# Decode block on one core: the first weight load as two half-partition loads on two queues

## The chip, the cores and the metric

The kernel runs on one core of a Trainium2 chip. The metric is device time in microseconds (us), the median of repeated runs; lower is better. The profile is of one execution.

## The reference

One decode step of a transformer block for 8 sequences, float32 throughout: a pre-norm grouped-query attention over the last 1,024 cached positions, then a pre-norm gated feed-forward part, both with residual additions.

```python
W = min(4096, max(256, Sk // 4))              # Sk = 4096, so W = 1024
q = (layernorm(x) @ wq)                       # x: 8 x 1024, wq: 1024 x 4096, 32 heads of 128
scores = q . k[last W] * Dh ** -0.5           # k, v: 8 x 4 x 4096 x 128, 8 query heads share a k head
o = softmax(scores) . v[last W]
h = x + o @ wo                                # wo: 4096 x 1024
g, u = layernorm(h) @ w_gate, layernorm(h) @ w_up     # 1024 x 3584 each
out = h + (gelu(g) * u) @ w_down              # 3584 x 1024
```

With 8 rows of activations, every weight and every cache line is read once and used for 8 rows: some 111 MB come in, and only 0.13 MB go out.

## The kernel before

The whole kernel is a stream of large loads from HBM into two equal buffers in SBUF, `w0` and `w1` (`wbuf`), each 128 partitions by 64 KB. Each load fills the buffers in turn: `wq` (two halves of the columns, `wq0` and `wq1`), `kt` (the transposed keys, two), `v` (two), `wo` (two), `gu` (gate and up weights, four), and `dn` with `ends` (the down weights, in pieces that get smaller towards the end). All loads are issued by SyncE (SP), in that order; the chip carries them out on 16 DMA engines. `load` gives a transfer a wait on the last matmul that reads the buffer (`free[i]`), so a load is issued as soon as the buffer's earlier content has been used, while the other buffer's load is still under way.

A load of 128 x 16384 floats is 8.39 MB; in the trace it is 128 packets of 64 KB, one for each partition, that is 8 for each of the 16 DMA engines.

There is no scheduler. `Flow.run` and `Flow.move` (line 87) issue instructions in the order in which the code is written, and put a semaphore wait ahead of an instruction where its engine has not yet seen the value that it needs. Each transfer has a semaphore of its own, which its landing raises by 16.

The start of the program, where the change lies, goes like this. SP issues `wq0` into `w0`, then `x` (8 partitions of 4 KB), then `wq1` into `w1`. VectorE (DVE) waits for `x`, takes its layer norm (lines 181 to 197, with one square root on ScalarE, ACT, line 188), TensorE (PE) transposes it (line 171), and DVE copies it out as `ln_t` (line 201). Then PE multiplies it by `wq0` into the PSUM bank `acc` (line 215, 32 matmuls, 64 in the trace's records), later by `wq1` into `tb`. The end of the first of these groups frees `w0`, and SP may issue `kt0`; the end of the second frees `w1` for `kt1`. From there on each stage has this form: a load lands, PE works through it, the buffer is free for the load after next.

Of the kernel before, what the change touches and what calls it, by code (L numbers as in the profile page):

```python
# [7 lines left out]
P = 128  # L8
# [6 lines left out]
NC = D // P  # L15
NQ = 4
# [17 lines left out]
class Flow:  # L34
# [42 lines left out]
    def run(self, engine, make, *waits, mark=True):  # L77
        ins = self.start(engine, make, waits)
        if not mark:
            return None  # L80
        self.done[engine] += 1
        ins.then_inc(self.own[engine], 1)
        return self.own[engine], self.done[engine]

    def move(self, name, out, src, *waits, engine="sync"):
        s = self.sem(name)
        self.start(engine, lambda e: e.dma_start(out, src), waits).then_inc(s, 16)  # L87
        return s, 16


def decode_block(nc, x, wq, kt, v, wo, gu, dn, ends, outs):
# [9 lines left out]
    run, move = fl.run, fl.move  # L101
# [4 lines left out]
    def sb(name, *shape):  # L106
        return nc.alloc_sbuf_tensor(name, list(shape), F32).ap()
# [9 lines left out]
    def buffer():  # L117
        i = turn[0] % 2
        turn[0] += 1
        return i, wbuf[i]  # L120

    def load(src, name, letters, **sizes):

        i, buf = buffer()
        n = 1
        for s in src.shape[1:]:
            n *= s
        t = buf[:, 0:n].rearrange(f"p ({letters}) -> p {letters}", **sizes)
        return t, move(name, t, src, free[i]), i
# [3 lines left out]
    acc = bank("acc", N)  # L133

    x_sb = sb("x_sb", B, D)
    wq_t = [load(wq[0], "wq0", "c n", c=NC)]
    x_in = move("x", x_sb, x)
    wq_t.append(load(wq[1], "wq1", "c n", c=NC))


    ident = sb("ident", P, P)
# [24 lines left out]
    def transposes(pt, src, n, ready, clear, rows=P):  # L166

        t = pt[:, 0:n * rows].rearrange("p (n r) -> p n r", n=n)
        tok = None
        for i in range(n):  # L170
            tok = run("tensor", lambda e, i=i: e.transpose(  # L171
                t[:, i, :], src[:, i * P:(i + 1) * P], ident[:rows, :rows]),
                id_ok, ready, clear, mark=(i == n - 1))
        return t, tok

    def layernorm_t(src, ready, name, clear):

        bn = sb(name + "_bn", B, D // N, 6)
        tok = None
        for i in range(D // N):  # L180
            tok = run("vector", lambda e, i=i: e.bn_stats(bn[:, i], src[:, i * N:(i + 1) * N]), ready)
        mv, ve, sd, r0, r1, r2, rs = (
            sb(f"{name}_{n}", B, k) for n, k in
            (("mv", 2), ("ve", 1), ("sd", 1), ("r0", 1), ("r1", 1), ("r2", 1), ("rs", 1))
        )
        tok = run("vector", lambda e: e.bn_aggr(mv, bn), tok)
        tok = run("vector", lambda e: e.tensor_scalar(ve, mv[:, 1:2], EPS, None, op0=ALU.add), tok)  # L187
        tok = run("scalar", lambda e: e.activation(sd, ve, AF.Sqrt), tok)  # L188
        tok = run("vector", lambda e: e.reciprocal(r0, sd), tok)

        tok = run("vector", lambda e: e.scalar_tensor_tensor(
            r1, r0, r0, ve, op0=ALU.mult, op1=ALU.mult), tok)
        tok = run("vector", lambda e: e.tensor_scalar(
            r2, r1, -0.5, 1.5, op0=ALU.mult, op1=ALU.add), tok)
        tok = run("vector", lambda e: e.tensor_mul(rs, r0, r2), tok)
        xn = sb(name + "_xn", B, D)
        tok = run("vector", lambda e: e.tensor_scalar(  # L197
            xn, src, mv[:, 0:1], rs, op0=ALU.subtract, op1=ALU.mult), tok)
        pt, tok = transposes(ta, xn, NC, tok, clear, B)
        xt = sb(name + "_t", P, NC, CP, B)  # L200
        tok = run("vector", lambda e: e.tensor_copy(  # L201
            xt, pt.unsqueeze(2).to_broadcast([P, NC, CP, B])), tok)
        return [xt[:, c].rearrange("p r b -> p (r b)") for c in range(NC)], tok

    xt, x_ok = layernorm_t(x_sb, x_in, "ln1", None)
# [4 lines left out]
    for hf in range(2):  # L210
        w, w_in, wb = wq_t[hf]
        q_ps = (acc, tb)[hf]
        for c in range(NC):
            for j in range(NQ):
                tok = run("tensor", lambda e, c=c, j=j: e.matmul(  # L215
                    q_ps[32 * j:32 * j + 32, :], xt[c], w[:, c, j * N:(j + 1) * N],
                    start=(c == 0), stop=(c == NC - 1)),
                    w_in, x_ok, mark=(c == NC - 1 and j == NQ - 1))
        free[wb] = tok
        q_sb = sb(f"q{hf}", P, N)  # L220
        tok = run("vector", lambda e: e.tensor_scalar(q_sb, q_ps, scale, None, op0=ALU.mult), tok)
        acc_free = tok
        qt, tok = transposes(ta, q_sb, N // P, tok, ta_free)

        for s in range(2):
            ta_free = run("vector", lambda e, s=s: e.tensor_copy(
                qz[hf][:, s].rearrange("p (b m) -> p b m", b=B)[:, :, 0:REP].rearrange(
                    "p b (k i) -> p b k i", k=2),
                qt.rearrange("p i (s k m) -> p s m k i", s=2, k=2)[:, s, 0:B]), tok, zero[hf])
        q_ok.append(ta_free)  # L230
# [3 lines left out]
    for hf in range(2):  # L234
        s_ps = big[hf]
        k_t, k_in, wb = load(kt[hf], f"kt{hf}", "s b k", s=2, b=B)
        for b in range(HB):
            for k0 in range(0, W, N):
                for r in range(NQ):
                    s, half = divmod(r, 2)  # L240
# [37 lines left out]
    for hf in range(2):  # L278
# [8 lines left out]
        for c in range(KC):  # L287
            for r in range(NQ):
                s, half = divmod(r, 2)
# [4 lines left out]
                    v_in, ta_free, ya_free, mark=(c == KC - 1 and r == NQ - 1))  # L294
# [15 lines left out]
    for hf in range(2):  # L310
# [3 lines left out]
        w, w_in, wb = load(wo[hf], f"wo{hf}", "h n", h=2 * REP)  # L314
# [26 lines left out]
    for k, nb in enumerate(SETS):  # L341
        pair = big[1 - k].rearrange("p (s n) -> p s n", s=2)
        clear = (ps[1][1], h_ok)[k]
        for s in range(2):
            w, w_in, wb = load(gu[k][s], f"gu{k}_{s}", "c n", c=NC)
            for c in range(NC):
                for j in range(nb):
# [3 lines left out]
                        w_in, ht_ok, clear, mark=(c == NC - 1 and j == nb - 1))  # L351
# [19 lines left out]
    for n in (HEAD, DF // P - HEAD):  # L371
        i, buf = buffer()
# [29 lines left out]
    for q in range(0, first, 2):  # L402
        for i in range(NQ):
# [7 lines left out]
                mark=(q == first - 2 and i == NQ - 1))  # L411
# [27 lines left out]
    mark = sb("mark", 1, 1)  # L439
# [82 lines left out]
```

## Time and profile before

| | us |
|---|---|
| median of 3 runs | 266.21 (266.11 to 266.24) |
| the profiled execution | 266.2 |
| its span, first to last instruction | 264.9 |
| busy PE / PE weight loads / DVE / ACT / GpSimd | 137.6 / 39.8 / 23.2 / 10.7 / 3.2 |
| first load issued, DVE begins on x | 0.74, 23.18 |
| wq1 landed, kt0 issued | 42.33, 37.90 |

The profile names DMA queues by numbers: q1 is the queue on which SP issues, q8 brings instructions in. "DMA share" in a row of a view by windows is the time of the packets that begin in the window, over 16 engines and the window's length; "GB/s" are the bytes of the same packets over the window's length. A packet is counted where it begins, so that a short window can show a share above 1, and share x length x 16 / number of packets is the mean time of one packet. `SPq` is SyncE's queue of transfers; a time "to landing" runs from issue to the semaphore of the transfer.

### The profile page before, as it was taken

To read this page: it belongs to the slowest core of one execution; us is meant where nothing else is said; L and a number is where in the kernel's file an instruction comes from. 1 tells how busy PE (TensorE), PEld (TensorE's weight loads), DVE (VectorE), ACT (ScalarE), POOL (GpSimd) and SP (SyncE) were. 2 spreads that over 40 slices of the span, in tenths; PEclk is the share of its full clock that TensorE was granted. 3 is DMA by queue.
4 is the path that set the end of the run, shared out by engine and by line. 5 is a ranking of instruction groups with operands and counts; after the bars stand their busy time and mean duration, and the time that the engine had idled before them with its cause. 6 is when DMAs were issued, how large, how long until landed. Compare 5 with 4: busy or idle time off the path is not lost.

```text
span 264.9 us, 2030 instructions
## 1 busy us (share of the span) xinstructions
PE 137.6 (52%) x946; PEld 39.8 (15%) x946; DVE 23.2 (9%) x55; ACT 10.7 (4%) x16; POOL 3.2 (1%) x11
## 2 busy tenths in 40 slices
PE   0000886804905906807707708719409585686696
PEld 0000321201201301302202202112102121121122
DVE  0004010100010020300200100260000200010001
ACT  1002000000010020110000000020000000000000
POOL 4000000000000000000000000000000000000000
PEclk9999997955965895965975956986966979599599
DMA  8998998999899989998999999999999998999994
GB/s 317 475 445 351 475 475 366 428 465 475 356 445 465 468 346 445 468 445 376 455 465 435 388 435 475 406 416 445 468 408 393 438 460 379 438 426 421 426 409 154
DMA packets 3192, 111.44 MB, mean 421 GB/s; under 512 B 360, under 2 KB 616, under 8 KB 1008
## 3 DMA queue, kind: packets, MB, share of 16 engines
q1 hardware_dynamic: 3184, 111.31, 97.9%
q8 instruction: 7, 0.11, 0.2%
q14 instruction: 1, 0.01, 0.0%
HBM read 111.18 MB, written 0.13 MB: 420 GB/s over the span
## 4 chain that ended last, share of the span: by engine, by line
DMA 75%; PE 22%; SPq 0%; issue 0%; DVE 0%; ACT 0%
DMA w<-gu 19%; DMA w<-wq 15%; DMA w<-kt 12%; DMA w<-wo 11%; DMA w<-v 11%; DMA w<-dn 8%; PE big L348 7%; PE big L243 4%; PE tb L290 3%; PE tb L215 3%; PE ya L318 3%; PE ya L406 1%; SPq L87 0%; DVE d L413 0%; ACT o_fin L437 0%
## 5 line engine op out<-in xcount | busy, mean ns | idle before, releaser
L348 PE MATMUL big<-w,ln_t 128*32 128x512 f32 x224 | 36.3, 734 | 21.6 <-DMA w<-gu 21.6
L243 PE MATMUL big<-w,qz 128*32 128x512 f32 x128 | 19.0, 762 | 20.5 <-DMA w<-kt 20.5
L318 PE MATMUL ya<-w,ot 128*32 128x512 f32 x128 | 18.2, 734 | 19.5 <-DMA w<-wo 19.5
L406 PE MATMUL ya<-w,at 128*32 128x512 f32 x104 | 17.4, 690 | 5.3 <-DMA w<-dn 5.3
L171 PE MATMUL ta<-ident,ln_xn 8*128 8x8 f32 x16 | 1.8, 236 | 31.7 <-DVE ln_xn L197 31.7
L348 PEld LDWEIGHTS big<-w,ln_t 128*32 128x32 f32 x224 | 9.1, 132 | 47.3 <-issue 26.0
L290 PE MATMUL tb<-w,pt 128*32 128x512 f32 x64 | 9.2, 741 | 9.7 <-DMA w<-v 9.7
L290 PE MATMUL acc<-w,pt 128*32 128x512 f32 x64 | 8.6, 700 | 8.5 <-DMA w<-v 8.5
L215 PE MATMUL tb<-w,ln_t 128*32 128x512 f32 x64 | 8.8, 711 | 3.1 <-DMA w<-wq 3.1
L243 PEld LDWEIGHTS big<-w,qz 128*32 128x32 f32 x128 | 4.9, 137 | 34.0 <-issue 23.4
L215 PE MATMUL acc<-w,ln_t 128*32 128x512 f32 x64 | 9.5, 761 | 0.5 <-DVE ln_t L201 0.5
L318 PEld LDWEIGHTS ya<-w,ot 128*32 128x32 f32 x128 | 5.0, 132 | 31.3 <-issue 31.3
L406 PEld LDWEIGHTS ya<-w,at 128*32 128x32 f32 x104 | 4.3, 124 | 17.5 <-issue 9.8
L171 PEld LDWEIGHTS ta<-ident,ln_xn 8*128 8x128 f32 x16 | 1.6, 188 | 32.6 <-DVE ln_xn L197 32.6
L359 DVE TENSOR_TENSOR hm<-ge,big 128x512 f32<-128x512 f32 (+1 forms) x2 | 1.4, 685 | 57.0 <-PE big L348 57.0
L252 DVE TENSOR_REDUCE nmax<-big 128x1 f32<-128x1024 f32 x2 | 2.4, 1224 | 36.3 <-PE big L243 36.3
L290 PEld LDWEIGHTS tb<-w,pt 128*32 128x32 f32 x64 | 2.6, 134 | 15.6 <-issue 15.6
L254 ACT ACTIVATE p<-big,nmax 128x1024 f32<-128x1024 f32 x2 | 2.2, 1114 | 65.9 <-DVE nmax L252 65.9
L290 PEld LDWEIGHTS acc<-w,pt 128*32 128x32 f32 x64 | 2.4, 126 | 14.1 <-issue 14.1
L188 ACT ACTIVATE ln_sd<-ln_ve 8x1 f32<-8x1 f32 x2 | 0.4, 203 | 84.0 <-DVE ln_ve L187 84.0
L215 PEld LDWEIGHTS tb<-w,ln_t 128*32 128x32 f32 x64 | 2.3, 127 | 8.8 <-issue 5.5
L215 PEld LDWEIGHTS acc<-w,ln_t 128*32 128x32 f32 x64 | 2.3, 135 | 7.0 <-issue 6.3
(72 smaller groups left out, 48.2 us busy)
## 6 DMA issues: line engine op xcount, KB each, us to landing
w<-gu SPq DMA_DIRECT2D x2, 6144.0 KB, 22.0
w<-dn SPq DMA_DIRECT2D x2, 4096.0 KB, 20.1
w<-dn SPq DMA_DIRECT2D x2, 2048.0 KB, 17.7
w<-dn SPq DMA_DIRECT2D x1, 1024.0 KB, 22.0
w<-dn SPq DMA_DIRECT2D x1, 512.0 KB, 22.8
w<-ends SPq DMA_DIRECT2D x2, 256.0 KB, 23.0
out<-o_fin SPq DMA_DIRECT2D x2, 64.0 KB, 1.6
w<-wq SPq DMA_DIRECT2D x2, 31.5
```

Of the source, the lines that this page charges most:

```text
L171: tok = run("tensor", lambda e, i=i: e.transpose(t[:, i, :], src[:, i * P:(i + 1) * P], ident[:rows, :rows]), id_ok, ready, clear, mark=(i ...
L188: tok = run("scalar", lambda e: e.activation(sd, ve, AF.Sqrt), tok)
L215: tok = run("tensor", lambda e, c=c, j=j: e.matmul(q_ps[32 * j:32 * j + 32, :], xt[c], w[:, c, j * N:(j + 1) * N], start=(c == 0), stop=(c ...
L243: tok = run("tensor", lambda e: e.matmul(s_ps[32 * r:32 * r + 32, k0:k0 + N], qz[hf][:, s, c0:c0 + 32], k_t[:, s, half * HB + b, k0:k0 + N ...
L252: tok = run("vector", lambda e: e.tensor_reduce(out=nmax, in_=s_ps, axis=AX.X, op=ALU.max, negate=True), tok)
L254: p_ok = run("scalar", lambda e: e.activation(p_sb, s_ps, AF.Exp, bias=nmax, accum_out=tot), tok)
L290: tok = run("tensor", lambda e: e.matmul(o3[32 * r:32 * r + 32], pt[:, c, 32 * r:32 * r + 32], v_t[:, s, c, half * HB:(half + 1) * HB, :], ...
L318: tok = run("tensor", lambda e: e.matmul(ya[32 * r:32 * r + 32, :], ot[:, 2 * hf * REP + h + e2].rearrange("p r b -> p (r b)"), w[:, h + e ...
L348: tok = run("tensor", lambda e: e.matmul(pair[32 * j:32 * j + 32, s, :], ht[c], w[:, c, j * N:(j + 1) * N], start=(c == 0), stop=(c == NC ...
L359: tok = run("vector", lambda e: e.tensor_mul(hm[:rows], ge[:rows], pair[:rows, 1, :]), tok, g_ok)
L406: tok = run("tensor", lambda e: e.matmul(ya[32 * r:32 * r + 32, :], at[:, q + e2, :], rows_of(q + e2)[:, ch * N:(ch + 1) * N], start=(q == ...
```

## The change

The first load, `wq0`, becomes two transfers: partitions 0 to 63 from SP's queue, partitions 64 to 127 from ACT's queue, both into the same buffer as before, each with a semaphore of its own. The first matmul on `wq0` waits for both. Nothing else is changed: `x` and `wq1` stay on SP, behind the first half now.

```diff
     x_sb = sb("x_sb", B, D)
-    wq_t = [load(wq[0], "wq0", "c n", c=NC)]
+
+    i, buf = buffer()
+    first_w = buf.rearrange("p (c n) -> p c n", c=NC)
+    half = P // 2
+    wq0_in = [move(f"wq0_{k}", first_w[k * half:(k + 1) * half], wq[0][k * half:(k + 1) * half],
+                   engine=("sync", "scalar")[k]) for k in range(2)]
+    wq_t = [(first_w, wq0_in, i)]
     x_in = move("x", x_sb, x)
-    wq_t.append(load(wq[1], "wq1", "c n", c=NC))
+    w1, w1_in, i = load(wq[1], "wq1", "c n", c=NC)
+    wq_t.append((w1, [w1_in], i))
...
                     q_ps[32 * j:32 * j + 32, :], xt[c], w[:, c, j * N:(j + 1) * N],
                     start=(c == 0), stop=(c == NC - 1)),
-                    w_in, x_ok, mark=(c == NC - 1 and j == NQ - 1))
+                    *w_in, x_ok, mark=(c == NC - 1 and j == NQ - 1))
```

ACT at the start of the program, before. A row is a line of the code, the operation, and what it writes from what; `ln_sd` is the square root in the layer norm, `p` the exponentials of the scores.

```order
L188 ACT_TABLE_LOAD
L188 ACTIVATE ln_sd<-ln_ve 8x1
L254 ACT_TABLE_LOAD
L254 ACTIVATE p,tot<-big,nmax 128x1024 x2
L284 COPY pt<-ya 128x512 x2
```

ACT at the same place with the change (the line numbers after the insertion are 7 higher):

```order
L87 DMA w<-wq 64x16384
L195 ACT_TABLE_LOAD
L195 ACTIVATE ln_sd<-ln_ve 8x1
L261 ACT_TABLE_LOAD
L261 ACTIVATE p,tot<-big,nmax 128x1024 x2
L291 COPY pt<-ya 128x512 x2
```

One transfer of 64 partitions now stands at the head of ACT's instructions, ahead of its first table load.

SP at the start of the program, with the change:

```order
L87 DMA w<-wq 64x16384
L87 DMA x_sb<-x 8x1024
L87 DMA w<-wq 128x16384
L87 DMA w<-kt 128x16384 x2
L87 DMA w<-v 128x16384 x2
```

Only the first row differs from before, where it was 128x16384; the order of SP's transfers is as it was.

## The prediction

> **What bounds the kernel now.** I read the page's DMA queues and the chain that ended last, then the chain in order of time, and then the first 60 us closely, since the change touches nothing behind them.
>
> The page's queues (packets, MB, share of 16 DMA engines over the span) and its chain:
>
> ```profile
> q1 hardware_dynamic: 3184, 111.31, 97.9%
> q8 instruction: 7, 0.11, 0.2%
> HBM read 111.18 MB, written 0.13 MB: 420 GB/s over the span
> DMA 75%; PE 22%; SPq 0%; issue 0%; DVE 0%; ACT 0%
> ```
>
> The DMA engines work 97.9% of the time. PE has 22% of the chain, but those are times in which the engines were loading something else. The start of the chain (start, length, what) shows how:
>
> ```profile
> 0.74 0.39 SPq L87
> ...
> 1.18 0.37 SPq L87
> ...
> 1.60 40.73 DMA w<-wq
> ...
> 42.37 8.81 PE tb L215 x64
> ...
> 51.20 31.07 DMA w<-kt
> ```
>
> SP issues `wq0` at 0.74, `x` at 1.18, `wq1` at 1.60, and `wq1` lands at 42.33 (1.60 + 40.73). The engines follow in the timeline (start, length, engine, line; in brackets what was waited for):
>
> ```profile
> 0.73 1.28 ACT L188 ACT_TABLE_LOAD   x1 [0.73 <-PEq L490]
> 23.18 1.27 DVE L181 BATCH_NORM_STATS2 ln_bn<-x_sb 8x6 f32<-8x512 f32 x2 [21.56 <-DMA x_sb<-x]
> 24.90 0.20 ACT L188 ACTIVATE ln_sd<-ln_ve 8x1 f32<-8x1 f32 x1 [22.89 <-DVE ln_ve L187]
> 28.31 9.52 PE L215 MATMUL acc<-w,ln_t 128*32 128x512 f32 x64 [0.52 <-DVE ln_t L201]
> 37.90 13.62 SPq L87 DMA_DIRECT2D w<-kt  x2
> ```
>
> `x` lands just before 23.18, PE works on `wq0` from 28.31 to 37.83, and `kt0` is issued at 37.90, 4.4 us before `wq1` has landed. So the DMA engines never run dry: PE could be some 3 us later at that place (4.4 less the 1.0 us that a transfer takes to begin, below) and nothing would change. What a stretch of the program costs is the time in which the DMA engines move its bytes; a time lost there goes to the end undiminished, and a time won elsewhere goes nowhere.
>
> How the engines move the first load is seen by windows (window, length, five engines, PE clock, DMA share, GB/s):
>
> ```profile
> 1.50:2.50 1.00, 0.00 (x0) 0.00 (x0) 0.13 (x1) 0.52 (x1) 1.00 (x3) 1.00 3.22 1049
> 1.70:2.20 0.50, 0.00 (x0) 0.00 (x0) 0.00 (x0) 0.32 (x1) 0.50 (x2) 1.00 6.44 2097
> 2.50:4.80 2.30, 0.00 (x0) 0.00 (x0) 0.00 (x0) 0.00 (x0) 1.28 (x3) 1.00 0.00 0
> 4.80:7.20 2.40, 0.00 (x0) 0.00 (x0) 0.00 (x0) 0.00 (x0) 0.00 (x0) 1.00 1.01 437
> ```
>
> 1049 GB/s for 1.00 us are 1.049 MB, that is 16 packets of 65,536 bytes: all 16 engines begin their first packet between 1.70 and 2.20, some 1.0 us after the issue, none begins one from 2.50 to 4.80, and all begin the next after that. They march in step, one partition's row at a time. A first packet takes 6.44 x 0.50 us = 3.22 us, a later one 1.01 x 2.40 = 2.42 us (27 GB/s for each engine). Eight of those are the load: 19.4 us.
>
> **The change part by part.**
>
> *The issue on ACT.* One transfer is added ahead of the table load at 0.73. A transfer's issue took SP 0.37 to 0.39 us whatever its size (8 partitions or 128). The table load then ends near 2.4 instead of 2.0, and ACT's next work is at 24.90: 22 us of cover. Cost 0; were the cover gone, 0.4. SP issues as many transfers as before; ACT's issue stands beside SP's, so both halves enter at about 0.74. Gain 0.
>
> *One more wait on PE*, ahead of the matmul at 28.31: some 0.05 us, in the 3 us of slack just named. 0. One more semaphore in the clearing at the end: 0.
>
> *x.* It stands behind 64 partitions of SP's queue instead of 128, but the other 64 go through the same 16 engines from ACT's queue. If the two take turns, `x` comes behind both as now; if it came earlier, `wq0`'s matmuls would end earlier than 37.83 and `kt0` would wait longer behind `wq1`. Gain 0 either way.
>
> *The bytes.* They are the same. I assume that the 64 rows of a half are dealt out to all 16 engines, 4 each, as 128 rows are now dealt out 8 each; then an engine has 4 packets from each queue, 8 as before. This is where the change can cost, in two ways.
>
> First, taking turns. The only other queue that breaks into the stream is q8, the instruction fetch. One of its packets (the row of the queues for 46.50 to 46.56, then of the stretch behind it):
>
> ```profile
> q8 instruction: 1, 0.02, 97.5%
> 47.40:47.50 0.10, 0.10 (x4) 0.00 (x0) 0.00 (x0) 0.00 (x0) 0.00 (x0) 1.00 1.82 655
> ```
>
> That fetch took 0.975 x 16 x 0.06 = 0.94 us for 16 KB, where a quarter of 2.42 would be 0.61; it begins at 46.5 and the next packet of an engine begins in the window at 47.4 and takes 1.82 x 0.10 x 16 = 2.91 us instead of 2.42. The two stand one behind the other, not inside one another, and a turn costs 0.33 us on the way in and 0.49 on the way back. With two queues an engine turns after each packet: 8 turns (the last to `x` and `wq1`) of 0.33 to 0.49 are 2.6 to 3.9 us. Bounds: 0 if the next packet of the other queue is fetched ahead as one of the same queue is, 3.9 if not. By itself I would take 3.3, nearest the rows.
>
> Second, where the rows go. Now, at any time, the 16 engines write to partitions out of all 128. With the change every engine's first packet is one of partitions 0 to 63 (or, if ACT is the first, of 64 to 127), and since they march in step and take turns by whole packets, all 16 are then in one half, then all in the other. Whether that costs depends on what sets the 27 GB/s: the engine, or the partitions' side of the path. No row tells these apart, since every large load spans 128 partitions and 16 engines at once; `x`, with its 8 partitions, is too small. Bounds: 0 if it is the engine; if it is the partitions' side, half of it takes half of 437 GB/s, the 8 packets of an engine take 4.84 us instead of 2.42, and the load 38.7 instead of 19.4: 19.4 more. Two engines that share a path are not quite in step: the 16 begin within 0.50 us (1.70 to 2.20), so two of them stand some 0.2 us apart, and that much of each packet runs alone: 8 x 0.2 = 1.6 less, 17.8. Turns may hide in it or come on top (up to 3.9). I take the upper end, 17.8, because the two conditions that the trace can show, step and whole packets, both hold.
>
> The Trainium skill, SBUF — State Buffer, section "Can I just issue two DMAs to hit both halves?", has a measurement of this: one transfer at partition 0 beside one at partition 64 came only 6% above a single one, and the section "Door 1: The DMA port swizzle (why `[64,N]` ≈ `[32,N]`)" gives 64 partitions 8 of 16 ports, some 218 GB/s. An estimate from that page is 8.39 MB at 231 GB/s, 36.3 us, which would make the sum +17; no run here shows it yet.
>
> *The sum.* Of the profiled execution: 264.9 + 17.8 = 282.7 of span, and the 1.3 us outside it (266.2 less 264.9, from these rows of the result) stay: 284.0. The profiled 266.2 is the median, 266.21, so this is also the forecast for the median.
>
> ```profile
> core 0: 264.9 us, clock 0.807
> ```
>
> The loss goes to the end whole: `x` would land near 41 (23.2 + 17.8), the `wq0` matmuls would end near 55.6, `wq1` would land near 60; the distance of 4.4 us is as before, and all later loads move by the same.
>
> **The rivals.**
>
> *Turns only* (slower, less). The rate is the engine's own, but each change of queue costs as the instruction fetch shows: 266.2 + 3.3 = 269.5, from 267.2 (two or three turns unhidden) to 270.1. For it: the 2.91 us packet. Against: the fetch is no weight load, and its turns may cost more than those between two weight loads.
>
> *Nothing* (the change doesn't do what it says: one stream is merely dealt out from two queues). 266.2, within 0.2%, which is 0.5 us and about what can be told from no change here. For it: 97.9%, the stream is full before and has the same bytes after. Against: it needs both the turns hidden and the partitions' side innocent. The Trainium skill, DMA: Bandwidth & Descriptors, section "Issuing engines are not separate DMA queues", says that transfers of several issuers run on the same 16 engines and that only issue time is saved; read alone, that is this case, and the issue times above leave nothing to save.
>
> *Faster.* The first packets take 3.22 us where later ones take 2.42: 0.8 us of start. If a packet of the second queue could be fetched during it, up to 0.8 would come back: 265.4. It decides only if turns are free and the two halves do not get in each other's way. Against: both first packets begin cold, and the 3.22 is paid once by each engine in either case. It is 0.8 at most, since behind the first packets the engines are full.
>
> **How the numbers follow.** Halves in each other's way: 0.50, since two of its three conditions are in the rows and the third is open; its own range is 274 to 289, the lower end where half the pairs of packets are out of step by a packet's width part of the time (8 us), the upper with the turns on top (17.8 + 3.9 = 21.7, 287.9, and a little). Turns only: 0.29. Nothing: 0.13. Faster: 0.08. Every one of the first two is over 0.2% slower, so 0.79 slower, 0.13 same, 0.08 faster. The range for 8 in 10 leaves out the last two and reaches from 267 to 289. The predicted time is that of the likeliest, 284.0.
>
> **What the profile after would show.** A second queue, of ACT, with 64 packets and 4.19 MB. In the windows from 1.7 on: under my forecast 16 packets of near 4.8 us each in step, some 220 GB/s to about 40 us, `x` read by DVE near 41, and from then on packets of 2.42 us; the share of the engines' time still near 98%, as they would be held, not idle. Under turns only: packets of 2.4 to 2.9 us, a share of a few hundredths less, DVE's first statistics near 26.5. Under nothing: 437 GB/s from 4.8 on as now, DVE near 23. In all of them the chain behind `wq1` should keep its lengths within 0.3 us.
>
> What would make it wrong: that the engines drift out of step early (one half of them in partitions 0 to 63 while the other is in 64 to 127, which costs nothing), that the two queues begin on different engines, that a packet of one queue is moved inside one of the other, or that a path to the partitions takes more than 27 GB/s.

## The result, and the profile after

The changed kernel takes 286.28 us (286.13 to 286.42, 4 runs) against 266.16 (266.03 to 266.24, 4 runs) of the kernel before, run beside it: a ratio of 1.0752, 95% interval 1.0739 to 1.0765, or 20.1 us more. The profiled execution took 286.42 us, with a span of 285.1.

The page after, DMA queues and chain (q10 is the new queue, ACT's):

```profile
q1 hardware_dynamic: 3120, 107.12, 90.9%
q10 hardware_dynamic: 80, 4.19, 7.0%
HBM read 111.18 MB, written 0.13 MB: 390 GB/s over the span
DMA 71%; PE 25%; DVE 2%; another core or an unknown queue 1%; issue 0%; SPq 0%; ACT 0%
```

q10's 80 packets are the 64 rows of the second half and 16 small ones, which begin between 41.0 and 42.6, where the load lands, and are taken to be those that raise its semaphore. Its 4.19 MB are 3.8% of the bytes but 7.0% of the engines' time: 0.070 x 16 x 285.1 / 64 = 4.99 us for a row, where a row took 2.42 before. The engines count as busy as before (90.9 + 7.0 = 97.9%); they are held, not idle.

The start of the chain after (start, length, what):

```profile
0.73 0.55 SPq L87
...
1.33 42.04 DMA x_sb<-x
...
43.40 1.29 DVE ln_bn L188 x2
...
48.53 9.15 PE acc L222 x64
...
57.70 0.70 DVE q L228
...
59.11 3.37 another core or an unknown queue
...
62.52 8.81 PE tb L222 x64
```

`x` reaches DVE at 43.40 (before 23.18: +20.2). The wait that ends at 62.48 is that of the matmuls on `wq1`. The chain does not name its source, but the page's row of these matmuls does:

```profile
L222 PE MATMUL tb<-w,ln_t 128*32 128x512 f32 x64 | 8.8, 711 | 3.4 <-DMA w<-wq 3.4
```

So `wq1` lands at 62.48, before at 42.33: +20.1. The span ends 20.2 later. So everything is lost before `x` lands, and nothing is lost or given back behind that.

How the engines move the first load after, by windows:

```profile
2.00:2.90 0.90, 0.00 (x0) 0.00 (x0) 0.00 (x0) 0.59 (x1) 0.90 (x2) 1.00 5.24 1165
2.90:6.30 3.40, 0.00 (x0) 0.00 (x0) 0.00 (x0) 0.00 (x0) 0.87 (x3) 1.00 0.00 0
6.30:7.40 1.10, 0.00 (x0) 0.00 (x0) 0.00 (x0) 0.00 (x0) 0.00 (x0) 1.00 4.54 953
11.30:12.40 1.10, 0.00 (x0) 0.00 (x0) 0.00 (x0) 0.00 (x0) 0.00 (x0) 1.00 4.51 953
16.30:17.40 1.10, 0.00 (x0) 0.00 (x0) 0.00 (x0) 0.00 (x0) 0.00 (x0) 1.00 4.51 953
```

Sixteen packets begin in each of these windows (1165 GB/s x 0.90 us and 953 x 1.10 are both 1.05 MB) and none from 2.90 to 6.30. They take 4.72, then 4.99, then 4.96 us (share x length). And within a window they are all of one queue, q1 in the first and the third, q10 in the second and the fourth; the queue's row for the second of these windows is

```profile
q10 hardware_dynamic: 16, 1.05, 453.8%
```

So the engines write 16 rows of partitions 0 to 63, then 16 rows of 64 to 127, in turn and in step, and each row takes twice its time.

### The profile page after: what moved, and what is told of

Read it like the earlier page. It is cut to its first block, busy times and chain, and to the rows that moved or that the text cites. A ratio compares the mean times of both kernels' runs of the same rounds, so it can differ in the third digit from the quotient of the medians.

```text
span 285.1 us, 2031 instructions
## 1 busy us (share of the span) xinstructions
PE 136.3 (48%) x946; PEld 39.7 (14%) x946; DVE 23.3 (8%) x55; ACT 10.7 (4%) x16; POOL 3.2 (1%) x11
## 3 DMA queue, kind: packets, MB, share of 16 engines
q1 hardware_dynamic: 3120, 107.12, 90.9%
q10 hardware_dynamic: 80, 4.19, 7.0%
## 4 chain that ended last, share of the span: by engine, by line
DMA 71%; PE 25%; DVE 2%; another core or an unknown queue 1%; issue 0%; SPq 0%; ACT 0%
DMA w<-gu 17%; DMA x_sb<-x 15%; DMA w<-kt 11%; DMA w<-wo 10%; DMA w<-v 10%; DMA w<-dn 7%; PE big L355 6%; PE ya L325 3%; PE big L250 3%; PE acc L222 3%; PE tb L222 3%; PE tb L297 3%; PE ya L413 1%; PE ta L178 1%; DVE ln_bn L188 0%
## 5 line engine op out<-in xcount | busy, mean ns | idle before, releaser
L355 PE MATMUL big<-w,ln_t 128*32 128x512 f32 x224 | 35.0, 711 | 21.0 <-DMA w<-gu 21.0
L325 PE MATMUL ya<-w,ot 128*32 128x512 f32 x128 | 19.0, 761 | 20.3 <-DMA w<-wo 20.3
L250 PE MATMUL big<-w,qz 128*32 128x512 f32 x128 | 18.3, 736 | 20.9 <-DMA w<-kt 20.9
L297 PE MATMUL acc<-w,pt 128*32 128x512 f32 x64 | 9.8, 782 | 9.2 <-DMA w<-v 9.2
L188 DVE BATCH_NORM_STATS2 ln_bn<-x_sb 8x6 f32<-8x512 f32 x2 | 1.3, 672 | 41.8 <-DMA x_sb<-x 41.8
## 6 DMA issues: line engine op xcount, KB each, us to landing
w<-dn SPq DMA_DIRECT2D x2, 4096.0 KB, 20.1
```

Source lines behind the costliest of these rows:

```text
L250: tok = run("tensor", lambda e: e.matmul(s_ps[32 * r:32 * r + 32, k0:k0 + N], qz[hf][:, s, c0:c0 + 32], k_t[:, s, half * HB + b, k0:k0 + N ...
L297: tok = run("tensor", lambda e: e.matmul(o3[32 * r:32 * r + 32], pt[:, c, 32 * r:32 * r + 32], v_t[:, s, c, half * HB:(half + 1) * HB, :], ...
L325: tok = run("tensor", lambda e: e.matmul(ya[32 * r:32 * r + 32, :], ot[:, 2 * hf * REP + h + e2].rearrange("p r b -> p (r b)"), w[:, h + e ...
L355: tok = run("tensor", lambda e: e.matmul(pair[32 * j:32 * j + 32, s, :], ht[c], w[:, c, j * N:(j + 1) * N], start=(c == 0), stop=(c == NC ...
```

## The experiments

All change only the lines that load `wq0`; the rest is the changed kernel. The reading that carries them is one window inside the first load: the mean time of a packet is DMA share x 16 x 65,536 bytes / rate. For comparison, before the change and after it:

```profile
7.00:19.00 12.00, 0.00 (x0) 0.00 (x0) 0.00 (x0) 0.00 (x0) 0.00 (x0) 1.00 1.01 437
```

```profile
7.00:37.00 30.00, 0.00 (x0) 0.00 (x0) 0.00 (x0) 0.00 (x0) 0.00 (x0) 1.00 1.06 225
```

That is 2.42 us for a packet before, and 4.94 after.

**One queue, or columns: is it the second queue or the halves?** `one_queue` keeps the halves and takes the second queue away:

```diff
-                   engine=("sync", "scalar")[k]) for k in range(2)]
+                   engine=("sync", "sync")[k]) for k in range(2)]
```

> Both halves of wq0 from SP's queue, the second behind the first; no second queue. If the partitions' side of the path is the limit (a half of the partitions takes writes at half the rate), the 128 packets still take near 4.95 us each, and the time is 266.2 + 8 x (4.95 - 2.42) = 286.4, or 0.3 less, since the two issues no longer stand beside each other: 286. If it is the turns between two queues that cost, there are none: 266.2.

`columns` keeps the two queues and takes the halves away:

```diff
-    half = P // 2
-    wq0_in = [move(f"wq0_{k}", first_w[k * half:(k + 1) * half], wq[0][k * half:(k + 1) * half],
+    half = NC // 2
+    wq0_in = [move(f"wq0_{k}", first_w[:, k * half:(k + 1) * half], wq[0][:, k * half:(k + 1) * half],
```

> wq0 still from two queues at once, SP's and ACT's, but split by its columns: each transfer has all 128 partitions, with rows of 32 KB. If the partitions' side is the limit, every packet has a partition group of its own as before the change, packets take near 1.21 us, and the time is 266.2 within 0.5. If turns between two queues cost, there are 16 for each engine, twice as many: at 0.33 to 0.49 us each 5 to 8 us more, 271 to 274; if they cost what the change cost, 286.

Measured: `one_queue` 287.1 us (1.0783, 1.0766 to 1.0801), `columns` 266.32 (1.0006, 0.9991 to 1.0020). The window from 7.00 to 37.00 of `one_queue`, then three windows of `columns`, in each of which 16 rows of 32 KB begin, in the first of ACT's queue, in the second of SP's, in the third of ACT's:

```profile
7.00:37.00 30.00, 0.00 (x0) 0.00 (x0) 0.00 (x0) 0.00 (x0) 0.00 (x0) 1.00 0.95 197
```

```profile
3.50:4.00 0.50, 0.00 (x0) 0.00 (x0) 0.00 (x0) 0.00 (x0) 0.27 (x1) 1.00 2.42 1049
4.70:5.20 0.50, 0.00 (x0) 0.00 (x0) 0.00 (x0) 0.00 (x0) 0.00 (x0) 1.00 2.43 1049
5.90:6.40 0.50, 0.00 (x0) 0.00 (x0) 0.00 (x0) 0.00 (x0) 0.00 (x0) 1.00 2.43 1049
```

Halves in one queue: 5.06 us a row, the loss is there without any turn between queues. Columns on two queues: 1.21 us a row of half the size, with a turn after each row, no loss. So the second queue is not what costs, and turns between two queues of weights cost nothing that shows.

**The middle: is it the number of partitions, or which?**

```diff
-    half = P // 2
-    wq0_in = [move(f"wq0_{k}", first_w[k * half:(k + 1) * half], wq[0][k * half:(k + 1) * half],
-                   engine=("sync", "scalar")[k]) for k in range(2)]
+    cuts = ((32, 96), (0, 32), (96, 128))
+    wq0_in = [move(f"wq0_{k}", first_w[a:b], wq[0][a:b]) for k, (a, b) in enumerate(cuts)]
```

> From SP's queue alone: first partitions 32 to 95, 64 of them as in the change but shifted by 32, then 0 to 31, then 96 to 127. If two halves 0-63 and 64-127 are the two sides of the path, the middle has half of each side: its 64 packets take 2.42 us, the 64 of the two outer pieces 4.95, and the time is 266.2 + 4 x 2.53 = 276.3. If a transfer of 64 partitions is slow as such, its packets take 4.95 too, and the time is 286 or more. If turns between queues were the cost: 266.2.

And with the rows that are read exchanged, which leaves the written side as it is (piece by piece: first partition, first row read, count):

```diff
+    cuts = ((32, 0, 64), (0, 64, 32), (96, 96, 32))
+    wq0_in = [move(f"wq0_{k}", first_w[a:a + n], wq[0][r:r + n]) for k, (a, r, n) in enumerate(cuts)]
```

> As the kernel with the middle first, but the rows that are read are exchanged: partitions 32 to 95 take rows 0 to 63 of wq0, that is the half that was read slowly; 0 to 31 take rows 64 to 95. The output is that of permuted weights. If the side that is written is the limit, this is like the middle: 276.3, packets 2.42 us in the first transfer. If the side that is read (these 4 MB of HBM) is the limit, its packets take 4.95 and the time is 286 or so.

Measured: 276.91 us (1.0403, 1.0388 to 1.0417) and 277.01 (1.0404, 1.0381 to 1.0426). Two windows of each, `middle` first: one while partitions 32 to 95 are written, one while the outer pieces are:

```profile
4.80:12.00 7.20, 0.00 (x0) 0.00 (x0) 0.00 (x0) 0.00 (x0) 0.00 (x0) 1.00 1.01 437
13.50:28.00 14.50, 0.00 (x0) 0.00 (x0) 0.00 (x0) 0.00 (x0) 0.00 (x0) 1.00 1.04 217
```

```profile
4.80:12.00 7.20, 0.00 (x0) 0.00 (x0) 0.00 (x0) 0.00 (x0) 0.00 (x0) 1.00 1.01 437
13.50:28.00 14.50, 0.00 (x0) 0.00 (x0) 0.00 (x0) 0.00 (x0) 0.00 (x0) 1.00 1.04 217
```

64 partitions are as fast as 128 if they are 32 to 95, and the rows that were slow into partitions 0 to 63 are fast into these. What limits is the side that is written, and which partitions they are.

**The middle on two queues: are packets moved one after the other?**

```diff
+    cuts = ((32, 96, "sync"), (0, 32, "scalar"), (96, 128, "scalar"))
+    wq0_in = [move(f"wq0_{k}", first_w[a:b], wq[0][a:b], engine=e) for k, (a, b, e) in enumerate(cuts)]
```

> Two queues, 64 partitions each: 32 to 95 from SP's queue, 0 to 31 and 96 to 127 from ACT's. If engines take turns by whole packets and in step, SP's packets take 2.42 us and ACT's 4.95, in turn, and the time is that of the same pieces from one queue, 276.9. If the two queues' packets ran beside each other, all paths would be in use most of the time, and the time would be nearer to 266.

Measured: 276.7 us (1.0389, 1.0368 to 1.0410). In one window 16 rows of SP's queue begin, in the next 16 of ACT's:

```profile
14.70:15.15 0.45, 0.00 (x0) 0.00 (x0) 0.00 (x0) 0.00 (x0) 0.00 (x0) 1.00 5.40 2330
17.10:17.55 0.45, 0.00 (x0) 0.00 (x0) 0.00 (x0) 0.00 (x0) 0.00 (x0) 1.00 10.75 2330
```

2.43 us, then 4.84: the queues take turns by whole rows, and what a slow row leaves idle is not used by the other queue.

**Smaller pieces, and spread pieces: what is a path?** A path here is what a group of partitions has in common when it is written, and what gives one engine alone its 2.42 us a row. From SP's queue, four pieces of 32 partitions in a row, or eight of 16:

```diff
+    cuts = [(a, a + 32) for a in range(0, P, 32)]
+    wq0_in = [move(f"wq0_{k}", first_w[a:b], wq[0][a:b]) for k, (a, b) in enumerate(cuts)]
```

> Four transfers of 32 partitions (0-31, 32-63, 64-95, 96-127) from SP's queue. If the rate goes with the number of partitions, a quarter of them has a quarter of the rate: packets of 9.9 us, 266.2 + 60 = 326. If partitions 32 apart share a path (each half of 64 has 8 paths, and so has each of its quarters): packets of 5.0 to 5.1, 286 to 288 as with halves.

> Eight transfers of 16 partitions each from SP's queue, one row for each engine. With four partitions to a path, 16 partitions reach 4 of 16 paths, four engines on each: packets near 9.9 us, eight of them 79 instead of 19.4, 326. Less if engines drift into the next transfer while others are still in the last one. If a transfer of under 128 partitions only pays a fixed price, it would be some 8 x 2.5 = 20 us at most: 286.

On the changed kernel's two queues, even partitions and odd ones:

```diff
+    wq0_in = [move(f"wq0_{k}", first_w[k::2], wq[0][k::2],
+                   engine=("sync", "scalar")[k]) for k in range(2)]
```

> Two queues again and 64 partitions each, but the even partitions from SP's queue and the odd ones from ACT's, so that both halves span all 128 partitions. If only the span counts (0-63 and 64-127 are the two sides): 266.2, packets 2.42 us. If paths belong to groups of four partitions, and the rows of a transfer are dealt out four in a row to each engine, then an engine's first two rows lie in one group of four and its next two in the following one, and at each moment only every second group is written, by two engines on each path: 286 again, packets 4.95.

And from SP's queue every fourth or every eighth partition, with `step` 4 or 8:

```diff
+    wq0_in = [move(f"wq0_{k}", first_w[k::step], wq[0][k::step]) for k in range(step)]
```

> Four transfers from SP's queue, each of every fourth partition (0, 4, 8 ... 124; then 1, 5, 9 ...): 32 partitions, as many as in the kernel with pieces of 32, but spread over all 128. If a path belongs to a group of four partitions (and to the group 32 further on), each transfer has rows on all 16 paths, two on each: 266.2, packets 2.42 us, if the rows are dealt to the engines so that two engines don't meet on a path. If they are dealt out two in a row to each engine, engines meet in pairs: 286. If only the span counts: 266.2.

> Eight transfers from SP's queue, each of every eighth partition (0, 8 ... 120; then 1, 9 ...): 16 partitions, as many as in the kernel with pieces of 16 (321.4), spread over all 128. With paths of four partitions, a transfer touches only every second group, 8 of 16 paths, two engines on each: packets near 4.95 to 5.1, 286. If only the span counts: 266.2. If the number of partitions counts: 321.

The window of `sixteen`, then that of `every_eighth`:

```profile
7.00:67.00 60.00, 0.00 (x0) 0.00 (x0) 0.00 (x0) 0.00 (x0) 0.00 (x0) 1.00 1.04 116
```

```profile
7.00:37.00 30.00, 0.00 (x0) 0.00 (x0) 0.00 (x0) 0.00 (x0) 0.00 (x0) 1.00 0.94 194
```

| one transfer covers | partitions | paths, if in fours and 32 apart shared | us | ratio (95%) |
|---|---|---|---|---|
| 0-15, 16-31 ... (`sixteen`) | 16 | 4 | 321.41 | 1.2068 (1.2044 to 1.2092) |
| every eighth | 16 | 8 | 287.23 | 1.0792 (1.0760 to 1.0823) |
| 0-31, 32-63 ... (`thirty_two`) | 32 | 8 | 286.84 | 1.0770 (1.0748 to 1.0791) |
| 0-63, 64-127, one queue | 64 | 8 | 287.10 | 1.0783 (1.0766 to 1.0801) |
| every fourth | 32 | 16 | 266.56 | 1.0011 (0.9999 to 1.0022) |
| every second, two queues | 64 | 16 | 266.42 | 1.0010 (0.9992 to 1.0028) |
| 32-95 (first piece of `middle`) | 64 | 16 | packets of 2.42 us | |

The time goes with the third column and not with the second: 16, 32 and 64 partitions all give 287 when they reach 8 paths, and 32 or 64 give 266 when they reach 16. "Only the span counts" falls with `every_eighth`, which spans all 128 and is slow. "The number of partitions counts" falls with `thirty_two` and `every_fourth`. The Trainium skill, SBUF — State Buffer, section "Door 1: The DMA port swizzle (why `[64,N]` ≈ `[32,N]`)", has this table of partitions and 16 ports, four partitions and the four 32 further on at one port; the ten experiments and the changed kernel agree with it. Four engines on a path: 1.04 x 16 x 65,536 / 116 GB/s = 9.4 us a row in `sixteen`; two: 4.94 to 5.08.

Three expectations missed in part. `one_queue` was expected 0.3 us below the changed kernel and came out 0.8 above it; a likely reason stands further on. `sixteen` took 321.4 us and 9.4 us a row instead of 326 and 9.9; the expectation named a reason, engines that are already in the next transfer, which was not tried by itself. And even and odd partitions ran at 266.4, where rows dealt out four in a row would have let engines meet in pairs. So rows are not dealt out that way there; how, these runs do not show.

## Why the prediction was right

*What bounds the kernel.* Right: the 20.1 us lost in the first load went to the end whole, with PE's and DVE's distances kept (`x` +20.2, `wq1` +20.1, span +20.2).

*Halves in each other's way.* Right in its mechanism, and this is the whole change: all three conditions hold. Step and whole packets are in the windows after; the third, which no row of before could tell, is settled by `columns`, `middle` and `middle_other_rows`: it is the written side, by paths. The bound was 19.4, the forecast 17.8; the kernel lost 20.1. The first packet took 4.72 instead of 3.22, the seven others some 4.95 instead of 2.42: 1.5 + 7 x 2.53 = 19.2. The forecast had counted all eight alike, at 2.22 (17.8 / 8). That the first cost only 1.5 made good 0.7 of what the seven others cost more, and this part of the nearness is luck. The prediction's other estimate, +17, took the load to run at 231 GB/s; 16 rows in 4.96 us are 211.

*Half the rate, and the 1.6 us taken off for engines out of step.* A row took 4.96 us, not 4.64 (4.84 less 0.2). The wrong term is the 4.84: two engines on a path got less than half the rate each. `one_queue` shows it in two windows, each of which holds one step of 16 rows. In the first the rows go to the same half of the partitions as the 16 before them; in the second the load goes over to the other half:

```profile
16.50:18.00 1.50, 0.00 (x0) 0.00 (x0) 0.00 (x0) 0.00 (x0) 0.00 (x0) 1.00 3.42 699
21.50:23.00 1.50, 0.00 (x0) 0.00 (x0) 0.00 (x0) 0.00 (x0) 0.00 (x0) 1.00 3.30 699
```

That is 5.13 us a row, and 4.95 at the change of halves. The trace has seven such steps behind the first: six take 5.12 or 5.13, and only this one less. `thirty_two` and `every_eighth` show the same: 5.12 to 5.13 before and after, 4.89 and 4.94 at the one step where they go over to the other eight paths. The changed kernel changes halves at every step, and its rows take 4.96. So a row on a shared path costs some 5.12 us, and a change of halves saves some 0.17 of it, near the 0.2 that the prediction took off. That engines out of step are the reason (the 16 packets begin over up to 1.1 us, 6.30 to 7.40) was not tried. It would also account for the 0.8 us that `one_queue` lies above the changed kernel: six steps without the saving are 6 x 0.17 = 1.0.

*Turns.* Wrong in size, 0 instead of 2.6 to 3.9: `columns` takes 16 turns an engine without loss. The slow instruction fetch and the slow packet behind it (0.94 and 2.91 us) were no price of a turn between two weight queues. The forecast had them outside its sum, so this moved only the ends of the range (289, and 267 by the rival) and gave the rival "turns only" a chance that it did not deserve.

*The issue.* 0 was right on ACT, whose table load began at 1.31 instead of 0.73 with its next work at 45.11. But an issue does not take the same time whatever its size, as the prediction had it: a half's takes 0.55 us where a whole's took 0.39, on SP too. The first packets begin some 0.3 later, of which this 0.16 is a part, and the sum lacked the term:

```profile
0.73 0.55 ACTq L87 DMA_DIRECT2D w<-wq  x1
1.31 1.28 ACT L195 ACT_TABLE_LOAD   x1 [1.31 <-PEq L497]
45.11 0.20 ACT L195 ACTIVATE ln_sd<-ln_ve 8x1 f32<-8x1 f32 x1 [42.52 <-DVE ln_ve L194]
```

19.2 and 0.3 are 19.5 of the 20.2 to `x`'s landing; the other 0.7 was not followed up.

*"Nothing"* failed on one of the two conditions named against it: the turns were hidden, but the partitions' side did set the rate. *"Faster"* had nothing to stand on: `columns`, where two queues start at once and no row is slowed, is not faster either.

## What to carry to other kernels

In these runs a transfer's rate was set by how many write paths its partitions reach, not by how many partitions it has or from how many queues it comes; split a load by columns, or by every second partition, and not into partitions 0 to 63 and 64 to 127. Before splitting a load across queues, ask whether anything waits for its issue: here the engines were at 97.9%, so even a good split (`columns`) brought nothing. And in this profile the sign was engines as busy as before with fewer bytes a second, in packets of double length: they were held by something that they share.

## What was not expected of the hardware

Two queues in turn lose nothing: rows of 32 KB from two queues alternate at 1.21 us each. Two engines that stay on a path get 2 x 65,536 bytes in 5.13 us, which is 25.6 GB/s, less than one engine alone takes from it (27.1). Four take 9.4 us a row in `sixteen`, which would be 27.9 GB/s if all four were on the path throughout; but there each transfer goes over to other paths, and the 16 rows of a step begin over some 2 us, so these runs do not show that a path gives more than 27.1. And issuing a half took 0.55 us, a transfer of all partitions 0.38 in `columns` with two queues issuing at once.
